# 776 instead of 756 score tiles on VectorE, with buffer rings that run on and a new written order

## The chip, the cores and the metric

The kernel runs on one core of a Trainium2 chip. The metric is device time in microseconds (us) of the whole program, as the median of several runs. The core has five engines that run their own instruction lists and wait for each other by semaphores: TensorE (PE in the profile, its weight loads PEld), VectorE (DVE), ScalarE (ACT), GpSimd (POOL) and SyncE (SP, which here only issues transfers).

## The reference

Two attention branches read the same input `x` of 2048 rows and 512 columns, with 32 heads of 16 dimensions. A gate `g = sigmoid(sum(x * gate_w))` per row mixes them.

```
A:  q,k,v = split(x @ wqkv);  pq = q @ w_phi;  pk = k @ w_phi        (per head)
    phi = concat(softmax(p), softmax(-p))
    o = phi_q @ (phi_k^T v) / (phi_q . sum(phi_k));   a = o @ wo      (linear attention)
B:  q,k,v = split(x @ wqkv);  p = softmax(q k^T / 4);  b = (p v) @ wo (full attention)
out = g * a + (1 - g) * b
```

Nearly all the time goes into B: for each of 32 heads a 2048 x 2048 score matrix, its exponential, and the product with `v`.

## The kernel before, in words

**Tiles and blocks.** B is cut into 32 blocks. A block is 512 query rows of four heads, which lie in four 32-row strips of the TensorE array. A block has 4 x 16 = 64 score tiles of 128 keys by 512 queries, 2048 tiles in all. TensorE makes a tile with one matmul (line 994: rows in the profile say `psS<-qz_t,kTB_t`, 32 rows by 128 columns of the array) into one of seven PSUM banks. Tiles of different heads use different row strips and stream together. The product with `v` (line 1136, `psO<-...,vaug_t`) uses 128 rows by 32 columns of the array; four of these on different column strips stream together into the bank `psO`. I call matmuls that stream together a round.

**Two ways to the exponential.** ScalarE takes two tiles at a time (line 1115, `E_t<-psS`, 128x1024) with its own exp; a tile then costs one product matmul. The other way is VectorE's: `max(s + EXPB, 0)` is written as a 16-bit integer (line 1084 for one tile, line 1074 for a pair of tiles in one instruction), and these bits, read as bf16, are a rough power of two. To smooth it, GpSimd adds a constant to all the integers, four at a time in a 64-bit add (line 1060, `INT64_ADD`), and later another one, and TensorE accumulates the product with `v` three times: of the first bits (`t`), of the first sum (`s`) and of the second (`m`). A tile on VectorE thus costs three product matmuls instead of one, and a quarter of two GpSimd adds, since up to four tiles form a group. `DN` (line 31) says how many tiles of each block go this way; there are 756, in 198 groups.

**Buffers.** A group uses a buffer for `t` and one for `s` and `m`. `PHASES` (line 32) lists rings of such buffers for three phases, from blocks 0, 16 and 27 on: `x0`, `x1` are halves of `Tx_t`, `y0`, `y1` of `Ty_t`, `a0` to `a3` lie in `vA_t`, `n0` in `WAT_t`, `wk`, `wq` in `Wp_t`, `wv` in `WB_t`. The loop behind it (lines 684 to 692) deals the buffers out in turn and starts at the ring's first buffer in each phase. A buffer can be written again when the TensorE matmuls that read it are done.

**The rest** is laid between: projections (line 754: 32 columns, line 842 and 855: V), branch A (transposes of line 1417, the two-operand VectorE operations `EA_t<-EA_t,ratio_t` of line 1444, `kzbd_t` of line 1473), each block's normalisation (copy of line 1231, small transfers by SyncE, `oT_t<-Tf_t,Rb_t` of line 1247), and the output projections at the end.

**The order** of each engine's instructions is written out by hand as numbers in `TABLE` (line 83), made offline; `Plan.place` (line 476) puts the operations in that order, gives each score tile the PSUM bank that `"homes"` names, and joins the VectorE operations of `"pairs"`. A -1 in TensorE's list is a filler: four matmuls with zero weights that add nothing (line 1126, `psO<-xT_t,zero_t`).

## Time and profile before

| | before |
|---|---|
| median of 3 runs, us | 659.53 (659.16 to 659.58) |
| profiled execution: span from first to last instruction, us | 657.6 |
| busy share PE / ACT / DVE / POOL, % | 99 / 97 / 93 / 62 |
| granted TensorE clock | 1.000 |
| exponentials of two tiles on ScalarE | 643 |
| VectorE score operations, single / pair | 638 / 59 |
| filler matmuls | 92 |

The span is one execution; the median contains 1.9 us more around it. PE's busy time counts each matmul until its modelled end, so that 99% says that matmuls follow each other closely, and not that the array streams all the time. How densely it streams is read from the starts of rows in the timeline.

### The profile page before, as it was taken

How to read it: one execution, taken by the hardware profiler on the slowest of the kernel's cores; microseconds unless marked ns; L12 is line 12 of the kernel's file. 1: busy time of each engine (PE TensorE's matmuls, PEld its weight loads, DVE VectorE, ACT ScalarE, POOL GpSimd, SP SyncE). 2: the span in 40 equal slices, each digit the busy share in tenths (PEclk: the TensorE clock that was granted, in tenths of full speed). 3: DMA queues.
4: the chain of work that ended last, by engine and by line, in shares of the span. 5: the costliest groups of instructions: out<-in, count | busy, mean ns of one | idle time of the engine just before them, and what ended most of it. 6: DMA issues, size and time to landing. Idle time of an engine off the chain costs nothing.

```text
span 657.6 us, 20651 instructions
## 1 busy us (share of the span) xinstructions
PE 649.1 (99%) x8820; PEld 227.3 (35%) x8820; DVE 609.4 (93%) x963; ACT 635.1 (97%) x720; POOL 410.8 (62%) x437
## 2 busy tenths in 40 slices
PE   8999999999999999999999999999999999999997
PEld 4333333434333333333233233322333333332333
DVE  6999899999998789999999999999999989999985
ACT  6999999999999999999999999999989999999996
POOL 7575367465665446486467876575867566656853
PEclk9999999999999999999999999999999999999999
DMA  6530101001010000000012431233211633134132
GB/s 131 104 100 12 33 12 27 11 11 19 11 27 10 16 18 8 19 17 14 23 37 47 100 77 33 63 78 68 48 51 35 102 56 83 35 63 103 44 84 48
DMA packets 67947, 30.94 MB, mean 47 GB/s; under 512 B 53208, under 2 KB 62808, under 8 KB 67856
## 3 DMA queue, kind: packets, MB, share of 16 engines
q1 hardware_dynamic: 65840, 28.82, 19.6%
q8 instruction: 69, 1.13, 0.7%
q10 hardware_dynamic: 1632, 0.79, 0.5%
q14 instruction: 22, 0.18, 0.1%
q0 software_dynamic: 384, 0.02, 0.1%
HBM read 7.87 MB, written 8.88 MB: 25 GB/s over the span
## 4 chain that ended last, share of the span: by engine, by line
PE 85%; DVE 12%; ACT 1%; issue 1%; DMA 1%; SPq 0%; DVEq 0%
PE psO L1136 32%; PE psS L994 30%; PE psS L754 15%; DVE Tx_t L1084 3%; PE psS L1417 3%; DVE Ty_t L1084 1%; DVE oT_t L1084 1%; DVE Wp_t L1084 1%; PE psS L842 1%; ACT E_t L1115 1%; DVE Tz_t L1084 1%; PE psS L1514 1%; PE psS L855 1%; PE psO L1126 1%; DMA phiK_t<-in_A_x_dram 1%
## 5 line engine op out<-in xcount | busy, mean ns | idle before, releaser
L1115 ACT ACTIVATE E_t<-psS 128x1024 bf16<-128x1024 f32 x643 | 601.9, 1068 | 11.2 <-PE psS L994 10.3
L994 PE MATMUL psS<-qz_t,kTB_t 32*128 32x512 bf16 (+1 forms) x2054 | 267.5, 383 | 2.8 <-ACT E_t L1104 0.6
L1084 DVE TENSOR_SCALAR Tx_t<-psS 128x512 int16<-128x512 f32 x246 | 163.2, 682 | 10.5 <-PE psS L994 9.4
L994 PEld LDWEIGHTS psS<-qz_t,kTB_t 32*128 32x128 bf16 x2054 | 71.8, 91 | 226.4 <-ACT E_t L1115 102.9
L1136 PE MATMUL psO<-E_t,vaug_t 128*32 128x512 bf16 x1292 | 119.0, 384 | 0.0
L1060 POOL INT64_ADD vA_t<-vA_t x72 | 71.6, 999 | 19.0 <-PE psO L1136 13.7
L1084 DVE TENSOR_SCALAR Ty_t<-psS 128x512 int16<-128x512 f32 x114 | 76.5, 682 | 4.8 <-PE psS L994 4.5
L1060 POOL INT64_ADD Ty_t<-Ty_t x42 | 44.0, 1048 | 18.5 <-PE psO L1136 18.1
L1060 POOL INT64_ADD Ty_t<-Tx_t x29 | 30.1, 1038 | 39.0 <-DVE Tx_t L1084 32.7
L1136 PE MATMUL psO<-vA_t,vaug_t 128*32 128x512 bf16 (+1 forms) x520 | 52.6, 384 | 0.0
L1136 PE MATMUL psO<-Ty_t,vaug_t 128*32 128x512 bf16 x440 | 45.4, 384 | 0.0
L1136 PEld LDWEIGHTS psO<-E_t,vaug_t 128*32 128x32 bf16 x1292 | 30.2, 95 | 39.5 <-issue 28.4
L1084 DVE TENSOR_SCALAR oT_t<-psS 128x512 int16<-128x512 f32 x62 | 41.7, 682 | 1.5 <-PE psS L994 1.0
L1084 DVE TENSOR_SCALAR Tz_t<-psS 128x512 int16<-128x512 f32 x60 | 40.2, 680 | 2.1 <-PE psS L994 1.8
L1060 POOL INT64_ADD vA_t<-Tx_t x22 | 22.7, 1032 | 31.0 <-DVE Tx_t L1084 24.1
L1060 POOL INT64_ADD phiQT_t<-Tx_t x19 | 18.9, 993 | 29.1 <-DVE Tx_t L1084 28.0
L1084 DVE TENSOR_SCALAR vA_t<-psS 128x512 int16<-128x512 f32 x54 | 36.2, 682 | 0.7 <-PE psS L994 0.3
L1084 DVE TENSOR_SCALAR WAT_t<-psS 128x512 int16<-128x512 f32 x52 | 35.2, 682 | 1.4 <-PE psS L994 1.2
L754 PE MATMUL psS<-Wp_t,xT_t 128*32 128x512 bf16 x512 | 35.8, 382 | 0.0
L754 PE MATMUL psS<-xT_t,WB_t 128*32 128x512 bf16 x480 | 34.9, 382 | 0.2
L1084 DVE TENSOR_SCALAR Wp_t<-psS 128x512 int16<-128x512 f32 x50 | 33.8, 683 | 0.9 <-PE psS L994 0.7
L1060 POOL INT64_ADD WoB_t<-oT_t x19 | 19.3, 1016 | 20.7 <-DVE oT_t L1084 16.5
(165 smaller groups left out, 920.1 us busy)
## 6 DMA issues: line engine op xcount, KB each, us to landing
dpq<-EA_t SPq DMA_DIRECT2D x16, 256.0 KB, 2.3
Rb_t<-lr SPq DMA_DIRECT2D x120, 32.0 KB, 1.9
dpo<-kv_t SPq DMA_DIRECT2D x16, 128.0 KB, 1.8
qz_t<-qz_t SPq DMA_DIRECT2D x120, 16.0 KB, 1.8
Tf_t<-Tf_t SPq DMA_DIRECT2D x60, 32.0 KB, 2.0
WB_t<-in_B_wqkv_dram SPq DMA_DIRECT2D x3, 384.0 KB, 3.6
out_dram<-WvA_t SPq DMA_DIRECT2D x8, 128.0 KB, 2.0
out_dram<-WB_t SPq DMA_DIRECT2D x6, 128.0 KB, 2.0
```

The costliest lines, as they stand in the source:

```text
L754: ins = e.matmul(out[32 * i:32 * i + 32, :], lhsT=lhsT[:, 32 * i:32 * i + 32], rhs=rhs, start=start, stop=stop, tile_position=(0, 32 * i))
L842: mms = [lambda e, ap, i=i, t=t: e.matmul(ap[:, 128 * i:128 * (i + 1)], lhsT=xT[:, t, NQ * c + 128 * i:NQ * c + 128 * (i + 1)], rhs=W_B[:, ...
L855: mms = [lambda e, ap, i=i, t=t: e.matmul(ap[:, 256 * i:256 * (i + 1)], lhsT=xT[:, t, NQ * c + 128 * (2 * hf + i):NQ * c + 128 * (2 * hf + ...
L994: return e.matmul(bank, lhsT=kT_B[32 * i:32 * i + 32, ROW[b // 2] % 2, 128 * kt:128 * (kt + 1)], rhs=qz[32 * i:32 * i + 32, b // 2 % 4, b ...
L1060: op = P.add("pool", P64 + W64 * size, d_prio(g["ts"][0]) - 5.0 + (0.0 if key == "s" else M_LATE), lambda e: e.int64_add(words(dst), words ...
L1084: ops.append(drain(f, mm, "dve", 0.70, d_prio(d), lambda e, ap, q=q: e.tensor_scalar(quarter(tb, q).bitcast(I16), ap, EXPB, 0.0, op0=ALU.a ...
L1115: op = P.add("act", EXP_OVH + 0.4267 * n, 0.0, lambda e: e.activation(Ebuf[:, j // 2 % EPAIRS, 512 * SZ[0] * (j % 2):512 * SZ[0] * (j % 2) ...
L1126: ins = e.matmul((psO if bank is None else bank)[32 * i:32 * i + 32, :], lhsT=zero[:], rhs=xT[:, 0, 0:NQ], start=bank is not None, stop=ba ...
L1136: return e.matmul(psO[32 * i:32 * i + w, :], lhsT=vaug[:, kt, o:o + w], rhs=rhs, start=start, stop=stop, tile_position=(0, 32 * i), skip_g ...
L1417: mms = [lambda e, ap, n=n, f=f: e.matmul(ap[:, 64 * n:64 * n + 64].rearrange("p (s g j) -> p s g j", s=2, j=4), lhsT=ident[:], rhs=es[n][ ...
L1514: mms = [lambda e, ap, g=g: e.matmul(ap[:, 64 * g:64 * g + 64], lhsT=qT(g)[:, 128 * j:128 * (j + 1)], rhs=kzbd[:, g, 0:64], start=True, st ...
```

## The change

Ten entries of `DN` grow by two, so that 20 more tiles go to VectorE (776 in 202 groups) and ten two-tile exponentials leave ScalarE. The rings no longer start anew with each phase: a group's place continues from the count of the phase before. All of `TABLE` is written anew; the title's last point, VectorE's operations with two operands in SBUF laid apart from GpSimd's adds, is in these numbers and in no other line of code.

```diff
-DN = (16, 24, 18, 24, 26, 26, 26, 20, 22, 22, 24, 18, 26, 24, 20, 26, 30, 22, 24, 26, 22, 24, 30, 26, 18, 22, 36, 18, 24, 24, 32, 16)
+DN = (16, 24, 18, 26, 26, 26, 28, 20, 22, 24, 24, 18, 28, 24, 20, 26, 32, 22, 26, 26, 22, 26, 30, 26, 20, 22, 36, 20, 24, 24, 34, 16)
...
+TURNS = (0, 0)
...
-    count = [0] * len(PHASES)
+    count, at = [0] * len(PHASES), [(0, 0)]
     for n, g in enumerate(groups):
         g["n"], g["ph"] = n, max(k for k in range(len(PHASES)) if g["ts"][-1]["t"][0] >= PHASES[k][0])
         rt, rs = PHASES[g["ph"]][1:]
         k = count[g["ph"]]
+        if g["ph"] == len(at):
+            more = count[g["ph"] - 1] - TURNS[g["ph"] - 1]
+            at.append(tuple((a + more) % len(ring) for a, ring in zip(at[-1], PHASES[g["ph"] - 1][1:])))
         count[g["ph"]] += 1
-        g["t"], g["s"] = rt[k % len(rt)], rs[k % len(rs)]
+        g["t"], g["s"] = (ring[(k + a) % len(ring)] for a, ring in zip(at[g["ph"]], (rt, rs)))
...
 TABLE = {
     "sp": (
-        0, 17, 2, 4, 5, 6, 7, 8, 10, 9, 11, 13, 14, 12, 15, 22, 26, 23, 27, 24, 25, 28, 29, 21, 132, 19, 967, 133, 968, 30, 20, 1094,
+        0, 17, 2, 4, 5, 6, 7, 8, 10, 9, 11, 12, 26, 13, 14, 15, 22, 21, 25, 28, 27, 24, 23, 30, 29, 19, 20, 132, 967, 133, 968,
...
```

What the new numbers do is seen in the built order. Instruction counts of the whole program that differ:

| | before | changed |
|---|---|---|
| ScalarE exponentials of two tiles | 643 | 633 |
| VectorE score operations, single / pair | 638 / 59 | 688 / 44 |
| GpSimd adds of four tiles / of two | 360 / 36 | 372 / 32 |
| product matmuls of 512 columns | 3560 | 3600 |
| filler matmuls | 92 | 0 |
| rounds of 512-column matmuls on TensorE | 2089 | 2065 |
| changes of the array's division (row strips, column strips, whole) between neighbours | 1215 | 1239 |

In the changed program code lines stand 14 to 17 further down (994 is 1011, 1136 is 1153, 754 is 768, 1060 is 1077, 1084 is 1101, 1417 is 1434).

First place, TensorE: the stretch before the transposes (`EA_t,ident_t`) of the fourth quarter of branch A's first query chunk. Before:

```order
L1136 MATMUL psO<-Tx_t,vaug_t 32x512 x4
L1136 MATMUL psO<-vA_t,vaug_t 32x512 x4
L994 MATMUL psS<-qz_t,kTB_t 128x512 x3
L1126 MATMUL psO<-xT_t,zero_t 32x512 x8
L994 MATMUL psS<-qz_t,kTB_t 128x512 x3
L1136 MATMUL psO<-Wp_t,vaug_t 32x512 x4
L1136 MATMUL psO<-vA_t,vaug_t 32x512 x4
L994 MATMUL psS<-qz_t,kTB_t 128x512 x4
L1136 MATMUL psO<-vA_t,vaug_t 32x512 x4
L994 MATMUL psS<-qz_t,kTB_t 128x512 x3
L1417 MATMUL psS<-EA_t,ident_t 128x64 x16
```

The same transposes in the changed program:

```order
L768 MATMUL psS<-xT_t,WB_t 32x512 x4
L1011 MATMUL psS<-qz_t,kTB_t 128x512 x4
L1153 MATMUL psO<-E_t,vaug_t 32x512 x6
L1153 MATMUL psO<-vA_t,vaug_t 32x512 x8
L1011 MATMUL psS<-qz_t,kTB_t 128x512 x3
L1531 MATMUL psS<-kzbd_t,phiQT_t 128x64 x4
L1531 MATMUL psS<-kzbd_t,WAT_t 128x64 x4
L1011 MATMUL psS<-qz_t,kTB_t 128x512 x2
L1531 MATMUL psS<-kzbd_t,phiQT_t 128x64 x4
L1531 MATMUL psS<-kzbd_t,WAT_t 128x64 x4
L1434 MATMUL psS<-EA_t,ident_t 128x64 x16
```

The filler pair (`zero_t`, two rounds) is gone, as are all 23 filler rounds, and other branch-A work stands close to the transposes; TensorE still alternates between score matmuls and products.

Second place, GpSimd: the first adds of the groups around block 27, where the third phase begins (a row names the buffer written and the one read; with different names it is a group's first add). Before:

```order
L1060 ISA vA_t<-Tx_t 128x1024 x2
L1060 ISA vA_t<-vA_t 128x1024
L1060 ISA WB_t<-Ty_t 128x2x256
L1060 ISA vA_t<-vA_t 128x1024 x3
L1060 ISA Ty_t<-Tx_t 128x1024
L1060 ISA vA_t<-WAT_t 128x1024
L1060 ISA vA_t<-vA_t 128x1024
L1060 ISA WB_t<-WB_t 128x2x256
L1060 ISA vA_t<-Tx_t 128x1024
```

Changed:

```order
L1077 ISA vA_t<-Wp_t 128x1024
L1077 ISA vA_t<-Tx_t 128x1024
L1077 ISA vA_t<-vA_t 128x1024 x2
L1077 ISA Wp_t<-WAT_t 128x4x256
L1077 ISA WB_t<-Tx_t 128x4x256
L1077 ISA Wp_t<-Wp_t 128x4x256
L1077 ISA Ty_t<-vA_t 128x1024
L1077 ISA WB_t<-WB_t 128x4x256
```

Before, the two last groups of block 26 and the two first of block 27 use both halves of `Tx_t`: each half comes up again two groups later, where the ring otherwise gives it back after six. Changed, the ring goes on with `Wp_t`, `Tx_t`, `Tx_t`, `WAT_t`, and each half comes up after six groups.

26 lines of the change are left out of this document (13 added, 13 removed), and 513 rows, old and new, of the table TABLE.

## The prediction

> **What bounds the kernel now.** I read the page's busy times first, then TensorE's timeline, since a busy share near 100% on three engines does not say which one sets the time.
>
> ```profile
> span 657.6 us, 20651 instructions
> PE 649.1 (99%) x8820; PEld 227.3 (35%) x8820; DVE 609.4 (93%) x963; ACT 635.1 (97%) x720; POOL 410.8 (62%) x437
> ...
> PE 85%; DVE 12%; ACT 1%; issue 1%; DMA 1%; SPq 0%; DVEq 0%
> ```
>
> The third row is the chain of work that ended last: 85% of it is TensorE, 12% VectorE, 1% ScalarE. GpSimd has room. What TensorE's share is made of shows in its timeline (start, length, what):
>
> ```profile
> 224.22 0.39 PE L1136 MATMUL psO<-oT_t,vaug_t 128*32 128x512 bf16 x4
> 224.43 0.39 PE L754 MATMUL psS<-Wp_t,xT_t 128*32 128x512 bf16 x4
> 224.65 0.39 PE L1136 MATMUL psO<-Tx_t,vaug_t 128*32 128x512 bf16 x4
> 224.97 0.39 PE L994 MATMUL psS<-qz_t,kTB_t 32*128 32x512 bf16 x3
> 225.29 1.12 PE L1417 MATMUL psS<-phiK_t,ident_t 128*128 128x64 bf16 x32
> 226.35 0.39 PE L994 MATMUL psS<-qz_t,kTB_t 32*128 32x512 bf16 x3
> ```
>
> Rounds of the same division of the array (rows of 128\*32) start 0.21 to 0.22 apart: 224.22, 224.43, 224.65. Where the next row divides it otherwise (128\*32 to 32\*128, or to 128\*128), the start comes after 0.32: 224.65 to 224.97 to 225.29. So a round is worth 0.22 and a change of division 0.10 more. The order of before holds 2089 rounds of 512 columns and 1215 changes: 2089 x 0.22 = 459.6 and 1215 x 0.10 = 121.5, together 581. The short matmuls come on top: 512 transposes in 16 runs of 32 at 1.06 each (225.29 to 226.35 above) are 17, and the V projections are 8 runs each of two kinds:
>
> ```profile
> 125.51 1.00 PE psS L842 x16
> ...
> 252.60 0.98 PE psS L855 x8
> ```
>
> These are 16 more; the small sums and products of branch A I estimate at 12 from their number. That is about 626 of 657.6. TensorE streams for 95% of the span with no waits counted, and under 30 is left for ramp, end and waits together. ScalarE is close behind:
>
> ```profile
> 93.16 19.52 ACT L1115 ACTIVATE E_t<-psS 128x1024 bf16<-128x1024 f32 x21
> ...
> L1115 ACT ACTIVATE E_t<-psS 128x1024 bf16<-128x1024 f32 x643 | 601.9, 1068 | 11.2 <-PE psS L994 10.3
> ```
>
> 21 exponentials in 19.52 with the last at its full 1.07: (19.52 - 1.07) / 20 = 0.92 from one to the next. ScalarE's idle time before them is 11.2 in all, and 10.3 of it ended with TensorE's scores. Among neighbours this tight TensorE leads: it is what ScalarE waits for, and it is the chain.
>
> **The change part by part.**
>
> *TensorE.* The fillers go:
>
> ```profile
> L1126 PE MATMUL psO<-xT_t,zero_t 128*32 128x512 bf16 x92 | 9.3, 384 | 0.0
> ...
> 423.28 0.62 PE L1126 MATMUL psO<-xT_t,zero_t 128*32 128x512 bf16 x8
> 423.83 0.45 PE L994 MATMUL psS<-qz_t,kTB_t 32*128 32x512 bf16 x3
> 424.21 0.40 PE L1136 MATMUL psO<-Wp_t,vaug_t 128*32 128x512 bf16 x4
> ```
>
> 92 are 23 rounds. Two of them hold the array from 423.28 to 423.83, which is 0.23 + 0.32, a round and a round with a change: the full price, with no idle time of TensorE ahead of the scores that follow. So these rounds are removed from a stream, 23 x 0.22 = 5.1. Against it stand 40 more product matmuls (20 tiles at three instead of one), ten rounds, and one more since a half-filled pair came in: 11 x 0.22 = +2.4. The same 2042 full score matmuls fall into 12 rounds fewer, -2.6. The divisions change 24 times more, 24 x 0.10 = +2.4. Sum: (-23 + 11 - 12) x 0.22 + 2.4 = -5.3 + 2.4 = **-2.9**. Bounds: if the fillers stood in time that TensorE would have waited anyway, the sum is -2.9 + 5.1 = +2.2 of work, paid out of waits; if the changes of division hide behind waits, it is -5.3. I take -2.9, since the row shows fillers paid in full.
>
> *ScalarE* loses ten exponentials, 10 x 0.92 = -9.2, from 635.1 to about 626. It gains nothing by itself as long as it waits for TensorE. If it set the pace everywhere the change would be worth up to 9.2.
>
> *VectorE* pays for it:
>
> ```profile
> 563.73 2.50 DVE L1084 TENSOR_SCALAR Tx_t<-psS 128x512 int16<-128x512 f32 x4
> ...
> 554.17 1.22 DVE L1074 TENSOR_SCALAR Wp_t<-psS 128x1024 int16<-128x1024 f32 x1
> 555.30 0.68 DVE L1247 TENSOR_TENSOR oT_t<-Tf_t,Rb_t 128x512 bf16<-128x512 f32 x1
> ```
>
> Single tiles follow each other at (2.50 - 0.68) / 3 = 0.61, and a pair holds it from 554.17 to 555.30, 1.13. 50 singles more and 15 pairs fewer: 50 x 0.61 - 15 x 1.13 = 30.5 - 17.0 = +13.5, or 0.42 for each of the 32 blocks. Its idle time of 657.6 - 609.4 = 48.2 covers that, but not evenly:
>
> ```profile
> 140.00:180.00 40.00, 39.87 (x592) 14.96 (x584) 39.51 (x59) 38.96 (x45) 24.49 (x28) 1.00 0.08 17
> ...
> 220.00:260.00 40.00, 40.00 (x566) 14.92 (x565) 34.49 (x51) 39.91 (x50) 21.65 (x26) 1.00 0.07 16
> 260.00:300.00 40.00, 39.83 (x543) 15.42 (x545) 39.06 (x60) 38.08 (x42) 24.43 (x26) 1.00 0.08 17
> 300.00:340.00 40.00, 39.08 (x528) 12.81 (x520) 38.66 (x65) 39.85 (x45) 26.24 (x26) 1.00 0.08 22
> 340.00:380.00 40.00, 39.92 (x526) 12.65 (x526) 39.05 (x61) 39.34 (x46) 28.50 (x29) 1.00 0.31 72
> 380.00:420.00 40.00, 39.88 (x552) 14.23 (x540) 38.72 (x62) 40.00 (x48) 27.15 (x27) 1.00 0.24 54
> ...
> 460.00:500.00 40.00, 39.87 (x557) 13.95 (x554) 38.80 (x63) 38.13 (x45) 29.02 (x30) 1.00 0.17 45
> ...
> 540.00:580.00 40.00, 39.88 (x559) 13.84 (x550) 38.94 (x63) 38.07 (x44) 25.32 (x26) 1.00 0.22 58
> ```
>
> (Columns: PE, PEld, DVE, ACT, POOL busy, then clock and DMA.) From 220 to 260 VectorE has 5.5 free of 40, but from 140 to 180 only 0.5, and from 260 to 300 and 340 to 380 0.9 each, where two blocks' addition is 0.84. I take 0 for the cover, with +4.1 for the whole program as the other end (worked out below as a rival).
>
> *GpSimd* gets 12 adds of four tiles and loses 4 of two:
>
> ```profile
> 557.88 0.61 POOL L1060 INT64_ADD WB_t<-Ty_t  x1
> ...
> 551.52 1.03 POOL L1060 INT64_ADD WB_t<-WB_t  x1
> ...
> 548.12 1.40 POOL L1060 INT64_ADD vA_t<-Wp_t  x1 [1.82 <-DVE Wp_t L1084]
> ...
> 547.93 0.68 DVE L1444 TENSOR_TENSOR EA_t<-EA_t,ratio_t 128x512 bf16<-128x512 bf16 x1
> ```
>
> 12 x 1.03 - 4 x 0.61 = +9.9 on 410.8, hidden in its 247 of idle time.
>
> *Two-operand operations apart.* The last two rows are a collision: the add at 548.12 begins while `EA_t<-EA_t,ratio_t` runs, and takes 1.40 instead of 1.03. GpSimd can afford that. VectorE pays in few places:
>
> ```profile
> L1247 DVE TENSOR_TENSOR oT_t<-Tf_t,Rb_t x15: 675/681/1200, 74.4 to 635.4; 128x512 bf16<-128x512 f32 x15
> ...
> 328.87 0.97 DVE kzbd_t L1473
> ```
>
> Of 15 normalisations (min/median/max in ns) the median is at the minimum and one took 1200, 0.52 over. The second row, from the chain of waits, is `kzbd_t`'s one operation, whose 0.97 stands against 0.60 between single-tile operations of equal size. At most 0.52 + 0.37 = 0.9 is to be had. I take **-0.4**, the part on the chain; 0 if the new order collides as often elsewhere. [...]
>
> *Rings.* At block 27 a `Tx_t` half is needed again after two groups instead of six. VectorE, which would wait for it, does not:
>
> ```profile
> 550.00:560.00 10.00, 9.88 (x142) 3.29 (x142) 10.00 (x14) 8.52 (x9) 8.09 (x9) 1.00 0.40 116
> ```
>
> It is busy all 10 of 10 there and TensorE 9.88, so TensorE can win 0.1; ScalarE's 1.5 of idle time ends up behind VectorE's own load. I take 0.
>
> Sum: -2.9 - 0.4 = -3.3, by the profiled execution 657.6 to 654.3. The median contains 1.9 more around the span, so **659.5 - 3.3 = 656.2**.
>
> **The rivals.** (1) *VectorE becomes the bound: slower.* Where it has no idle time left, each block grows by 0.42 instead of shrinking by 3.3 / 32 = 0.10. With n such blocks the change is 0.42 n - 0.10 (32 - n): zero at n = 6, and +1.3 at n = 9. The seven windows quoted with under 1.4 of 40 idle hold 14 blocks, at 20.5 each: 5.9 - 1.8 = +4.1, so 663.6. For it: VectorE's 12% of the chain. Against it: the new order may move VectorE's other work out of these stretches, and its whole idle time, 48.2, is 3.6 times the addition. (2) *ScalarE is the true bound: much faster.* Then all of 9.2 counts, 650.3. For it stand its 97%; against it, its idle time is ended by TensorE and it has 1% of the chain. [...] The starts above, 0.22 and 0.32 apart without gaps, speak against it. (3) *Nothing to be measured:* the fillers stood where waits now open, and TensorE's additional 2.2 is paid from ScalarE's slack, within 1.3 of 659.5. For it: behind the two fillers at 423.28 the product of 424.21 starts 0.38 after its scores instead of 0.32, so a wait of 0.06 follows them all the same. Against it: 0.06 is little beside 0.45. That the separation does not happen at all is part of it: it costs 0.4.
>
> **How the numbers follow.** Forecast 0.54, with its own range 654.2 (-5.3) to 658.2 (a gain of 1.3); rival 1 0.17; rival 2 0.08; rival 3 0.21. About 0.2% (1.3) can be told from no change. Faster: 0.54 + 0.08 = 0.62; same 0.21; slower 0.17. The range 652.0 to 661.5 leaves out most of rival 2 and over half of rival 1.
>
> **What would show it.** Right: the same 0.22 and 0.32 in TensorE's timeline, no `zero_t` rows, TensorE still over 80% of the chain, VectorE's busy time near 623 and ScalarE's near 626, no add of GpSimd over 1.1. Wrong: VectorE's share of the chain well over 12% with windows at 39.5 of 40 (rival 1); score matmuls waiting for VectorE where fillers stood (rival 3); TensorE idle and a gain near 9 (rival 2).

## The result: 8.6 us slower

| | before | changed |
|---|---|---|
| median, us | 659.56 (659.16 to 660.84) | 668.18 (667.01 to 671.1) |
| ratio to before | | 1.0132, 95% interval 1.0106 to 1.0159 |
| profiled execution, span, us | 657.6 | 665.0 |
| mean granted clock | 1.000 (profiled execution) | 1.000, 0.997, 0.995, 0.990 (the four timed executions; the first is the profiled one) |

The forecast was 656.2, the range 652.0 to 661.5. The time lies above both, and above the 663.6 of the rival on VectorE. The page of the changed kernel (span, busy times, the chain of work that ended last, the exponentials):

```profile
span 665.0 us, 20578 instructions
PE 649.9 (98%) x8768; PEld 228.1 (34%) x8768; DVE 620.9 (93%) x998; ACT 630.4 (95%) x710; POOL 422.6 (64%) x445
...
PE 66%; DVE 11%; SPq 10%; ACT 7%; DMA 3%; issue 1%; DVEq 0%
...
L1132 ACT ACTIVATE E_t<-psS 128x1024 bf16<-128x1024 f32 x633 | 595.4, 1042 | 23.6 <-PE psS L1011 22.7
```

TensorE's part of the chain falls from 85% to 66%. What takes its place is not VectorE (12% before, 11% now) but SyncE's queue (SPq, from 0 to 10%), ScalarE (1 to 7%) and the transfers themselves (1 to 3%). These shares tell where the path runs and not what a stretch costs: by line, 4 of SyncE's 10% are turned loads of the start (L696 and L706, loads that transpose on the way). ScalarE waits for scores twice as long as before, 23.6 instead of 11.2.

To see where TensorE lost time, I took the distance from each of its rounds to the next, and subtracted the lower quartile of the distances between rounds of the same kinds in the kernel before. The quartiles' sum is TensorE's work, the rest its waits. By this the work is 625.3 before and 622.5 now: -2.8, where -2.9 was forecast. The waits went from 27.8 to 38.0. Up to 400 us they are about the same (20.7 and 19.9). After 400 us, in us and by the engine that ended them:

| waits of TensorE after 400 us, ended by | before | changed |
|---|---|---|
| VectorE | 3.7 | 9.9 |
| ScalarE | 1.0 | 2.8 |
| a transfer | 0.0 | 1.8 |
| GpSimd | 0.1 | 1.4 |
| nothing that the trace shows | 2.3 | 2.2 |

VectorE's rise does not hang on how a wait is put down to an engine; GpSimd's does (by the releaser of each round's first matmul it has 0.3 before and now). Of these waits 0.9 is in pieces over 250 ns before, and 8.8 now. A few long waits are new. They are followed one by one.

**Transfers that land late.** The first two are at the start. TensorE's timeline of the changed kernel:

```profile
32.11 0.38 PE L1393 MATMUL psS<-Wbp_t,WAT_t 128*128 128x128 bf16 x4 [1.71 <-DMA WAT_t<-in_A_wqkv_dram]
...
35.26 0.38 PE L1393 MATMUL psS<-Wbp_t,WAT_t 128*128 128x128 bf16 x4 [0.92 <-DMA WAT_t<-in_A_wqkv_dram]
```

These products need the eight turned loads of `WAT_t` (`DMA_TRANSPOSE` in the rows). SyncE issues one after the other; seven of the eight stand here. Its queue in the changed kernel:

```profile
20.08 1.26 SPq L706 DMA_TRANSPOSE WAT_t<-in_A_wqkv_dram  x1
21.39 0.58 SPq L703 DMA_DIRECT2D WB_t<-in_B_wqkv_dram  x1
22.01 8.41 SPq L706 DMA_TRANSPOSE WAT_t<-in_A_wqkv_dram  x5
30.47 0.58 SPq L708 DMA_DIRECT2D WvA_t<-in_A_wqkv_dram  x1
31.10 1.19 SPq L706 DMA_TRANSPOSE WAT_t<-in_A_wqkv_dram  x1
```

and in the kernel before, where all eight stand together and the first product came 4 us later:

```profile
18.84 11.41 SPq L692 DMA_TRANSPOSE WAT_t<-in_A_wqkv_dram  x8
```

In the changed kernel two loads that nobody waits for yet stand between them, and the products were moved ahead.

The second half has the other ones. A block's row sums travel from VectorE's copy of the result (`Tf_t<-psO`) through memory (`ld`, then `Lq_t`) back to VectorE's reciprocal, and that one's result through memory again (`lr`, then `Rb_t`) to the scaling. Blocks are normalised in pairs. Pair 25 in the kernel before, VectorE first, then SyncE's queue:

```profile
535.85 0.68 DVE L1231 COPY Tf_t<-psO 128x512 f32<-128x512 f32 x1
543.80 0.34 DVE L1240 RECIPROCAL rd_t<-Lq_t 128x32 f32<-128x32 f32 x1
555.30 0.68 DVE L1247 TENSOR_TENSOR oT_t<-Tf_t,Rb_t 128x512 bf16<-128x512 f32 x1
```

```profile
536.56 0.53 SPq L1233 DMA_DIRECT2D ld<-Tf_t  x1
538.28 0.34 SPq L1235 DMA_DIRECT2D Lq_t<-ld  x1
...
544.17 0.38 SPq L1242 DMA_DIRECT2D lr<-rd_t  x1
...
547.08 5.03 SPq L1244 DMA_DIRECT2D Rb_t<-lr  x8
```

And in the changed kernel:

```profile
538.19 0.68 DVE L1248 COPY Tf_t<-psO 128x512 f32<-128x512 f32 x1
...
544.67 0.35 DVE L1257 RECIPROCAL rd_t<-Lq_t 128x32 f32<-128x32 f32 x1 [0.97 <-issue]
...
557.32 0.81 DVE L1264 TENSOR_TENSOR oT_t<-Tf_t,Rb_t 128x512 bf16<-128x512 f32 x1 [1.38 <-DMA Rb_t<-lr]
```

```profile
537.66 1.85 SPq L913 DMA_DIRECT2D qz_t<-qz_t  x3
539.56 1.26 SPq L1506 DMA_TRANSPOSE phiQT_t<-dpq  x1
540.92 0.53 SPq L1250 DMA_DIRECT2D ld<-Tf_t  x1
541.51 1.13 SPq L1506 DMA_TRANSPOSE phiQT_t<-dpq  x1
542.68 0.57 SPq L1252 DMA_DIRECT2D Lq_t<-ld  x1
...
547.37 0.38 SPq L1259 DMA_DIRECT2D lr<-rd_t  x1
547.80 1.19 SPq L1506 DMA_TRANSPOSE WAT_t<-dpq  x1
549.03 1.25 SPq L1506 DMA_TRANSPOSE phiQT_t<-dpq  x1
550.33 5.26 SPq L1261 DMA_DIRECT2D Rb_t<-lr  x8
```

Before, `ld` is issued 0.03 after the copy, and `Lq_t` has landed 3.8 ahead of the reciprocal. Now `ld` stands 2.05 behind the copy's end: copies of `qz_t` and a turned read of `dpq`, whose user comes at 562, stand ahead of it, one more turned read ahead of `Lq_t`, and two more ahead of `Rb_t`. VectorE waits 0.97 and 1.38. (The first row says "issue" since the profile names no releaser; `Lq_t` landed at 544.59, 0.08 ahead of that row's start.) It waited for no transfer before. TensorE is held up behind it: from the scores at 544.71 to the next at 545.62 it takes 0.91, and from 557.45 to 558.79 it takes 1.34, of which the trace shows 0.53 and 0.95 as idle, both ended by VectorE's operations on score tiles (`vA_t`, L1101). It needs the banks of score tiles that VectorE had not got to.

For the whole list I compared each transfer's landing with the start of its first user on TensorE or VectorE; I call the time between them the margin. Leaving out the first 24 us, of SyncE's 214 transfers with such a user none lands less than 1.0 us ahead in the kernel before, and 20 do in the changed kernel, 10 of them less than 0.3. The counts depend on how a transfer is paired with its user: with only those users whose own tile the transfer writes they are 0 and 12. From the end of a pair's copy to its reciprocal the median is 7.3 us before (6.7 to 9.4) and 5.4 now (4.2 to 11.7).

### The profile page after: what moved, and what is told of

It is laid out like the page before. It is cut to its first block, busy times and chain, and to the rows that moved or that the text cites. A ratio compares the mean times of both kernels' runs of the same rounds, so it can differ in the third digit from the quotient of the medians.

```text
span 665.0 us, 20578 instructions
## 1 busy us (share of the span) xinstructions
PE 649.9 (98%) x8768; PEld 228.1 (34%) x8768; DVE 620.9 (93%) x998; ACT 630.4 (95%) x710; POOL 422.6 (64%) x445
## 4 chain that ended last, share of the span: by engine, by line
PE 66%; DVE 11%; SPq 10%; ACT 7%; DMA 3%; issue 1%; DVEq 0%
PE psO L1153 26%; PE psS L1011 23%; PE psS L768 12%; ACT E_t L1132 7%; DVE Tx_t L1101 3%; SPq L1506 2%; SPq L696 2%; PE psS L1434 2%; SPq L706 2%; PE psS L869 1%; SPq L1261 1%; DVE vA_t L1101 1%; DVE Ty_t L1101 1%; DVE WAT_t L1101 1%; DVE EA_t L1461 1%
## 5 line engine op out<-in xcount | busy, mean ns | idle before, releaser
L1132 ACT ACTIVATE E_t<-psS 128x1024 bf16<-128x1024 f32 x633 | 595.4, 1042 | 23.6 <-PE psS L1011 22.7
L1101 DVE TENSOR_SCALAR Tx_t<-psS 128x512 int16<-128x512 f32 x262 | 172.1, 681 | 4.9 <-PE psS L1011 4.2
L1153 PE MATMUL psO<-E_t,vaug_t 128*32 128x512 bf16 x1272 | 125.5, 384 | 0.0
L1101 DVE TENSOR_SCALAR Ty_t<-psS 128x512 int16<-128x512 f32 x116 | 77.5, 680 | 4.8 <-PE psS L1011 4.3
L1153 PE MATMUL psO<-vA_t,vaug_t 128*32 128x512 bf16 x534 | 53.1, 385 | 0.0
L1101 DVE TENSOR_SCALAR Tz_t<-psS 128x512 int16<-128x512 f32 x72 | 47.9, 680 | 1.2 <-PE psS L1011 0.6
L1101 DVE TENSOR_SCALAR oT_t<-psS 128x512 int16<-128x512 f32 x66 | 43.7, 682 | 1.0 <-PE psS L1011 0.6
L1101 DVE TENSOR_SCALAR vA_t<-psS 128x512 int16<-128x512 f32 x62 | 41.3, 679 | 0.6 <-PE psS L1011 0.4
L768 PE MATMUL psS<-Wp_t,xT_t 128*32 128x512 bf16 x512 | 40.9, 382 | 0.5 <-DMA dpq<-EA_t 0.5
L1101 DVE TENSOR_SCALAR Wp_t<-psS 128x512 int16<-128x512 f32 x58 | 38.9, 680 | 1.4 <-PE psS L1011 1.4
L1077 POOL INT64_ADD Ty_t<-Tx_t x24 | 24.0, 1002 | 23.9 <-DVE Tx_t L1101 23.4
L1101 DVE TENSOR_SCALAR WAT_t<-psS 128x512 int16<-128x512 f32 x52 | 34.7, 682 | 0.9 <-PE psS L1011 0.8
L1077 POOL INT64_ADD WoB_t<-oT_t x19 | 18.9, 996 | 22.3 <-DVE oT_t L1101 21.6
L1077 POOL INT64_ADD WoA_t<-Tz_t x19 | 20.2, 1063 | 15.0 <-DVE Tz_t L1101 11.4
L1077 POOL INT64_ADD vA_t<-Tx_t x22 | 22.0, 1002 | 11.7 <-DVE Tx_t L1101 11.5
```

Source lines behind the costliest of these rows:

```text
L768: ins = e.matmul(out[32 * i:32 * i + 32, :], lhsT=lhsT[:, 32 * i:32 * i + 32], rhs=rhs, start=start, stop=stop, tile_position=(0, 32 * i))
L1077: op = P.add("pool", P64 + W64 * size, d_prio(g["ts"][0]) - 5.0 + (0.0 if key == "s" else M_LATE), lambda e: e.int64_add(words(dst), words ...
L1101: ops.append(drain(f, mm, "dve", 0.70, d_prio(d), lambda e, ap, q=q: e.tensor_scalar(quarter(tb, q).bitcast(I16), ap, EXPB, 0.0, op0=ALU.a ...
L1132: op = P.add("act", EXP_OVH + 0.4267 * n, 0.0, lambda e: e.activation(Ebuf[:, j // 2 % EPAIRS, 512 * SZ[0] * (j % 2):512 * SZ[0] * (j % 2) ...
L1153: return e.matmul(psO[32 * i:32 * i + w, :], lhsT=vaug[:, kt, o:o + w], rhs=rhs, start=start, stop=stop, tile_position=(0, 32 * i), skip_g ...
```

## The experiments

The theories were: the load of VectorE (rival 1 of the prediction), SyncE's queue, the fillers (rival 3), and, after the first runs, the granted clock and the margins as a whole. Medians are of all timed executions; the mean granted clock of single executions is given where it matters, and "at the full clock" means 1.000. In 56 executions of the kernel before that clock was under 0.9985 once.

| run | median, us (lowest to highest) | ratio to before, 95% |
|---|---|---|
| e1 no fillers | 659.93 (658.6 to 661.1) | 0.9997, 0.9989 to 1.0006 |
| e2 VectorE's load on before | 671.21 (670.8 to 671.3) | 1.0170, 1.0157 to 1.0184 |
| e3 VectorE relieved | 671.15 (667.4 to 674.2) | 1.0177, 1.0151 to 1.0202 |
| e4 queue mended | 665.62 (660.5 to 666.1) | 1.0067, 1.0041 to 1.0093 |
| e5 start only | 670.40 (667.8 to 671.6) | 1.0156, 1.0133 to 1.0179 |
| e6 later queue only | 666.53 (663.4 to 668.9) | 1.0098, 1.0075 to 1.0120 |
| e7 fillers for the clock | 666.68 (663.9 to 673.7) | 1.0119, 1.0081 to 1.0156 |
| e8 queue and fillers | 665.07 (664.0 to 671.1) | 1.0094, 1.0064 to 1.0125 |
| e9 margins by hand | 667.54 (666.0 to 668.6) | 1.0115, 1.0101 to 1.0128 |
| e10 margins and fillers | 669.27 (667.5 to 674.4) | 1.0153, 1.0125 to 1.0180 |
| e11 margins taken from before | 665.56 (663.2 to 666.2) | 1.0084, 1.0071 to 1.0097 |
| e12 e9 with VectorE relieved | 666.59 (665.9 to 668.9) | 1.0108, 1.0095 to 1.0122 |
| e13 row-sum block in before | 662.24 (659.8 to 665.0) | 1.0028, 1.0013 to 1.0044 |
| e14 searched queue and fillers | 664.94 (664.5 to 666.2) | 1.0070, 1.0054 to 1.0086 |

### The fillers

e1, the kernel before without its fillers, one of 23 places (this diff and some later ones have the operations' names in place of `TABLE`'s numbers):

```diff
-  dq21.13.3.0, qk424, -1, dq21.13.0.0
+  dq21.13.3.0, qk424, dq21.13.0.0
```

> The kernel before with its 23 filler rounds struck from TensorE's written order and nothing else changed. The prediction's first term (each filler takes a whole round of TensorE's time, 23 x 0.22 us): 5.1 us less, about 654.4. The prediction's third rival (the fillers stood in time in which TensorE waited anyway): within 1.3 us of before, 658.2 to 660.9. The theories on what the change cost (VectorE's load, SyncE's queue) say nothing of this run.

No change: 0.9997, which with its interval is between 0.7 us faster and 0.4 slower. The answer of rival 3 holds. The prediction had read the full price from two fillers at 423.28; this is the same place in TensorE's timeline without them:

```profile
422.26 0.39 PE L994 MATMUL psS<-qz_t,kTB_t 32*128 32x512 bf16 x3
423.09 0.46 PE L994 MATMUL psS<-qz_t,kTB_t 32*128 32x512 bf16 x3 [0.43 <-ACT E_t L1115]
423.48 0.40 PE L1136 MATMUL psO<-Wp_t,vaug_t 128*32 128x512 bf16 x4
```

Between the two scores there were 0.87 (422.96 to 423.83) with the fillers and there are 0.83 without. A wait for ScalarE's exponential came into their place. By the count of the first section TensorE's work fell by 6.2 over the program, and its waits rose by 5.4. In 4 of the 11 executions the clock's mean was 0.997; the section on the clock comes back to that.

### VectorE's load

e2, the kernel before with 22 single score tiles worked twice:

```diff
+            def score(e, ap, q=q, twice=twice):
+                if twice:
+                    e.tensor_scalar(spare[:], ap, EXPB, 0.0, op0=ALU.add, op1=ALU.max)
+                return e.tensor_scalar(quarter(tb, q).bitcast(I16), ap, EXPB, 0.0, op0=ALU.add, op1=ALU.max)
```

> The kernel before with 22 single score tiles of VectorE worked twice, the second time into a spare tile that nobody reads: about 13.1 us more work on VectorE, in the order of before, with the same result and no other engine's list touched. Theory of VectorE's load (the prediction's first rival: with 0.42 us more for each block VectorE is the bound): 4 us or more slower, 663.5 to 672. Theory of SyncE's queue (the new order puts other transfers ahead of those that are waited for, and the load by itself costs little): less than 2 us slower, below 661.5.

11.6 us slower, for 12.1 more of VectorE's busy time (621.5). Its chain, and the row of the added operations:

```profile
PE 70%; DVE 27%; issue 1%; ACT 1%; DMA 1%; SPq 0%; DVEq 0%
...
L1091 DVE TENSOR_SCALAR spare_t<-psS 128x512 int16<-128x512 f32 x22 | 15.0, 684 | 0.5 <-PE psS L994 0.5
```

VectorE's share rises from 12% to 27%. That answers the theory of the load, for this order: where the order isn't laid for it, VectorE's time is paid almost in full, and 48 us of idle time in sum cover 0.5 of 12.1. (The added operation stands ahead of the real one, so it also puts each of the 22 tiles off by some 0.6; load and delay are not told apart.) But the changed kernel has the same busy time (620.9) without this share in its chain. Its order was laid anew for the load, and so the other direction was to be tried on it.

e3, the changed kernel with 26 single tiles written for 64 of 512 queries:

```diff
-                quarter(tb, q).bitcast(I16), ap, EXPB, 0.0, op0=ALU.add, op1=ALU.max),
+                quarter(tb, q)[:, 0:w].bitcast(I16), ap[:, 0:w], EXPB, 0.0, op0=ALU.add, op1=ALU.max),
```

> The changed kernel, in its own order, with 26 of VectorE's single score tiles after the first 64 written for 64 of their 512 queries only (what the others of these tiles hold is left from before, so that part of the scores is left out): about 12 us less work on VectorE, every wait and transfer as it was. Theory of VectorE's load: the loss goes, 659 to 661. Theory of SyncE's queue: the waits for transfers stay, at most 2 us of the 8.6 come back, 666 or more.

671.15: nothing came back in the median, with 8.9 us less of VectorE's busy time (612.0; a short tile still takes 0.20 to 0.22, a full one 0.68). The clocks of its six executions are 0.984 to 0.995, lower than the changed kernel's, so some of what it gained may be hidden; e12 below repeats it on another basis. Even so the theory of the load as the one cause, which had 659 to 661, is not borne out.

### SyncE's queue

e4, the changed kernel with the written order mended (the numbers of `TABLE`; in SyncE's list 13 to 15 are loads of `x`, 22 to 29 those of `WAT_t`, 21 and 30 the two that were in between):

```diff
-  26, 13, 14, 15, 22, 21, 25, 28, 27, 24, 23, 30, 29, 19, 20
+  13, 14, 15, 22, 25, 24, 23, 26, 28, 27, 29, 21, 30, 19, 20
...
-  582, 3511, 581, 624, 626, 584, 583
+  582, 581, 584, 624, 626, 3511, 583
...
-  3645, 629, 3646, 628, 3647, 3649, 3650, 3822
+  3645, 3646, 3647, 3649, 629, 3650, 628, 3822
...
-  700, 3691, 4439, 701, 4568, 699, 4569, 4570, 4277, 4572, 705, 702, 4573
+  700, 4439, 701, 4568, 4569, 4570, 4572, 4573, 699, 705, 702, 3691, 4277
...
-  777, 4888, 772, 776, 773
+  777, 772, 776, 773, 4888
```

The second edit lets the scaled queries (624, 626) go ahead of a reordering of queries that is needed 80 us later; the third and fourth put the row sums of pairs 19 and 25 (3645 to 3650, 4568 to 4573) ahead of turned reads (628, 629, 699, 702, 705) and stores; the fifth puts a store behind turned reads. In TensorE's list product 243 moves behind 509 and 505, and VectorE's evictions follow.

> The changed kernel with SyncE's written order mended in five places and nothing taken out: at the start the six bias and weight loads that TensorE does not wait for stand behind the eight it does (and one of the weight products that need the last of these stands behind two that need the first four); in the second half the writes and reads of the row sums, the gathers of the merged outputs and the writes of the scaled queries stand ahead of the transposes and stores that nobody waits for yet. VectorE's work is as in the changed kernel. Theory of SyncE's queue: the five stalls of TensorE that the trace of the changed kernel puts down to transfers (2.9 us at the start, 0.7, 0.5, 0.9, 1.3 and 1.1 us later) go, 6 to 8 us less, 660 to 662. Theory of VectorE's load: VectorE was late anyway and its other waits take their place, at most 2 us less after the start's 2.9, 663 or more.

Its trace has none of these waits for transfers any more. The executions fall into two groups: 660.53 and 661.98 at a clock of 1.000, and 665.4 to 666.1 at 0.988 to 0.995. At the full clock it is 5.0 to 6.5 below the changed kernel's 667.01, what SyncE's theory forecast, and within 0.4% of the kernel before. The median, 665.62, is 2.6 below. So two things seem to work here; the second is the clock.

e5 has the first edit and TensorE's alone, e6 the four later ones:

> The changed kernel with the start alone mended: on SyncE the biases and the weight load that are not waited for stand behind the eight loads of the transposed weight, and the weight product that needs the last of them stands behind two that need the first four. Theory of SyncE's queue: the stalls of 1.87 and 0.99 us at 30 and 34 us go, and the executions at the full clock lie 2.9 us lower, at 664.1. If the start is made up for later (another engine is late anyway): within 1 us of the changed kernel's 667.0. The clock's theory (next run) says that the executions spread upwards by 2 to 5 us as those of the changed kernel do.

> The changed kernel with SyncE's order mended in the four later places alone (from 410 us on) and the start as it was. Theory of SyncE's queue: stalls of 0.7, 0.5, 0.9, 1.3 and 1.1 us go, the executions at the full clock lie 3.6 to 4.5 us lower, at 662.5 to 663.4. Theory of VectorE's load: VectorE is late at these places without the transfers too, less than 1.5 us. Together with the run before the two gains should come to the 6.5 us by which the fastest execution of the kernel with both lies below the changed kernel's fastest.

e6 at the full clock has 663.39, 3.6 less, as forecast. e5 has no execution at the full clock (0.989 to 0.994), so its time decides nothing. Its trace says more: TensorE is 2.2 us earlier than in the changed kernel from 36 us on and still at 382 us, and 2.7 earlier at 612. It loses 3.5 right after that: it waits 2.1 for the turned reads, 1.0 more than in the changed kernel, and then the clock is at half from 616 to 623. The start is not made up for by another engine, but a lead is no use where the next transfer is not earlier too.

All this sets single executions against a single one, the 667.01, and the same list is not equally late in each execution. e7 below has the SyncE list of the changed kernel, and at the full clock it has 663.88 and 667.11. In its profile neither operation of pair 25 waits:

```profile
543.24 0.34 DVE L1261 RECIPROCAL rd_t<-Lq_t 128x32 f32<-128x32 f32 x1
...
554.55 0.68 DVE L1268 TENSOR_TENSOR oT_t<-Tf_t,Rb_t 128x512 bf16<-128x512 f32 x1
```

At the start the last `WAT_t` lands at 35.12 in the changed kernel's profile, and at 33.44, 34.04 and 34.44 in those of e3, e6 and e7 with the same list there; with the mended one it lands at 31.13 and 31.30 (e4, e5). So the order of the list decides how late a transfer can be, and the execution how late it is. What the mended list is worth is therefore better read from all executions: the ratio is 1.0067 against 1.0132, and the intervals do not overlap (up to 1.0093, from 1.0106). That is about half of the loss, some 4 us.

### The granted clock

The profiled execution of e4 around its first group of row-sum products, the products of 4 columns with `kzbd_t` in branch A (columns: PE, PEld, DVE, ACT, POOL busy, then the clock and DMA):

```profile
384.00:388.00 4.00, 3.12 (x64) 1.60 (x56) 3.97 (x9) 3.09 (x4) 3.00 (x3) 1.00 0.19 38
388.00:392.00 4.00, 4.00 (x34) 0.70 (x32) 3.42 (x6) 3.51 (x4) 2.15 (x3) 0.65 0.28 88
392.00:396.00 4.00, 4.00 (x38) 0.71 (x34) 2.52 (x5) 2.53 (x4) 1.04 (x1) 0.50 0.46 138
```

The clock is at half for some 7 us, and only 34 to 38 matmuls start in 4 us, where the two windows of 4 us behind have 60 and 50. By the rows that is (0.35 + 0.50) x 4 = 3.4 us of full speed; by the starts of the same rounds TensorE lost 2.9 us there against the changed kernel's profile. In the 4 us ahead TensorE stands still for 0.9 in three pieces (0.40, 0.15, 0.33), and among the rounds between are 32 products of 4 columns. The changed kernel's own profiled execution has the same stretch at the full clock; its other executions have 0.990 to 0.997. The same fall shows in the profiles of e3, e6, e9 and e12, at 386 to 389, and others in e3, e5, e6 and e10 after 616, behind the wait for the last turned reads.

e7 puts fillers there (five around the first group, four in the wait ahead of the last), e8 puts them into e4:

```diff
+  -1, -1, 3306, 3462, 3370, 3464, 3304, -1, 563, 564, -1, 565, 566, -1, 3467
-  3306, 3462, 3370, 3464, 3304, 563, 564, 565, 566, 3467
```

> The changed kernel with nine filler rounds (0.22 us each, all zeros, the same as those of the kernel before) put into the stalls around two groups of rounds that hardly stream: five around the first group of row-sum products at 384 to 387 us, where TensorE waits 0.40, 0.15 and 0.33 us between rounds of 4 columns, four in the stall of 1.1 us before the last group at 616 us. SyncE's order as in the changed kernel. Theory of the clock (the granted clock falls to half for some 7 us when a stretch of about 3 us holds too little streaming, as in the traces of the two last runs after 388 and after 619 us): no execution under a mean clock of 0.998 but for the start, and the executions lie close together at 667 +- 1. If the fall of the clock has another cause: the same spread from 667 to 671 with clocks of 0.990 to 0.995.

> The changed kernel with SyncE's order mended at the start and in the later places, and seven filler rounds around the first and the last group of row-sum products. If late transfers and the fallen clock are all that this order lost against its own full-clock demand: 660.0 to 661.5 in nearly all executions, level with the kernel before at 659.6 to within 0.3%. If the clock falls for another reason: the two groups of times seen without the fillers, near 661 and near 666.

In the profiles of all four runs with fillers at the first group (e7, e8, e10, e14) the clock does not fall there; in five of the seven profiles of the changed order without them it does. By the starts of the same rounds the five fillers cost TensorE 0.46 us there in the profiles of e7, e8 and e14. But the spread stayed (0.987 to 1.000 in e7, 0.990 to 1.000 in e8), since it falls elsewhere: in e7 after a wait of 1.6 us for VectorE, ended at 590.8. And e8 is not level with the kernel before, as was expected: at the full clock it has 664.0 and 664.5. In its trace TensorE waits 1.5 us for a copy of the queries at 44 us (`qe0.1`), which landed 0.7 ahead of its user in the profile of the changed kernel, and 0.8 at 647 us for a turned read. The executions are late at different places.

e13 asks the question by itself, in the kernel before:

```diff
-  Z0.0, dq19.15.1.0, qk390, Z0.8, Z0.16, Z0.24, dq19.14.2.0, qk391, -1
+  Z0.0, Z0.8, Z0.16, Z0.24, dq19.15.1.0, qk390, dq19.14.2.0, qk391
```

(three more -1 within 15 us of it are struck out too).

> The kernel before with the first group of row-sum products (four rounds of 4 columns, at 397 us) in one piece, as the changed kernel has it, instead of one round, two other rounds and three, and with the four filler rounds around it struck out; all else as before. Theory of the clock (a stretch with little streaming at this place makes the granted clock fall to half for some 7 us): in at least a third of the executions a mean clock of 0.995 to 0.997 and 2 to 4 us more, the others at 659.7. If the block and the fillers have nothing to do with it: all executions at 0.999 or more and 659.7 +- 0.5, as those of the kernel before.

Ten of twelve executions have a clock of 0.992 to 0.997 and 661.4 to 665.0, and the two others 659.8 and 659.9. That is what the theory of the clock had said. The profile shows the place, and for comparison the same stretch of the kernel before:

```profile
402.00:406.00 4.00, 3.22 (x27) 0.99 (x31) 3.83 (x8) 3.67 (x5) 2.25 (x2) 0.60 0.01 2
406.00:410.00 4.00, 4.00 (x57) 1.23 (x45) 3.10 (x5) 2.98 (x5) 2.17 (x3) 0.97 0.05 12
```

```profile
402.00:406.00 4.00, 4.00 (x61) 1.33 (x53) 4.00 (x6) 4.00 (x6) 2.27 (x3) 1.00 0.04 10
406.00:410.00 4.00, 4.00 (x55) 1.12 (x54) 4.00 (x6) 4.00 (x5) 3.43 (x4) 1.00 0.35 113
```

In these 8 us the clock lacks (0.40 + 0.03) x 4 = 1.7 us of full speed. The run changes the block and four fillers together. e1 answers this in part: with all fillers out and the block as it was, the clock is 0.997 in 4 of 11 executions, against one in 56 with the fillers. So taking fillers out is part of it, and fillers, which the prediction had as a cost alone, also held up the clock here. The profile has a second fall, at 7 to 14 us, where e4's has one too.

What sets the clock was not shown. In all nine profiles that have a fall (e3 to e7, e9, e10, e12 and e13) the lowest clock of any 2 us is 0.50. The stretch of about 3 us in e7's expectation is, in e4's trace, the one that holds the three pieces, 384.44 to 387.32; how long such a stretch must be, or how little TensorE must do in it, was not measured.

### The margins

e11 takes from the kernel before what the changed one lacks. Only VectorE's list changes, pair 19 for example:

```diff
-  ev.19 and 12 others, rd19
+  ev.19 and 7 others, rd19, the 5 others
```

> The kernel before with one thing changed: the reciprocal of the row sums stands two to six places earlier on VectorE in thirteen of the fifteen pairs of blocks, so that it comes about 5.2 us after the eviction that its input sets out from, the distance that the changed kernel has, instead of 7.3. All engines' work, all transfers and their order as before. Theory of the margins: VectorE waits for the landing in some of the pairs (1 to 2 us in pair 19, under 1 us in 23, what the landings vary by in others), 1 to 3 us slower with a wider spread, 660.5 to 663. If the transfers' margins do not matter: within 0.7 us of the kernel before.

5.9 us slower, twice the upper end of what I expected, and 3.5 to 4.2 at the full clock (663.19 and 663.87). VectorE's wait at pair 19 (its `Lq_t` landed 0.08 ahead of the row's start), and TensorE's behind it:

```profile
427.70 0.35 DVE L1244 RECIPROCAL rd_t<-Lq_t 128x32 f32<-128x32 f32 x1 [1.94 <-issue]
```

```profile
428.66 0.64 PE L1421 MATMUL psS<-EA_t,ident_t 128*128 128x64 bf16 x16 [1.92 <-DVE Tx_t L1088]
```

1.94 of VectorE become 1.92 of TensorE: there is no cover on the way. Three of five executions have a clock of 0.995 to 0.997; that these falls follow the late transfers is not shown, since the profiled execution has none. This run moves only small operations by 2 to 4 us, with the load, the transfers and their order as they were.

e9 was to give the changed kernel margins, by hand, e10 the fillers too, and e12 repeats the relief of e3 on e9 (26 single tiles written for 64 of 512 queries):

```diff
-  ld0, qe0.1, lq0
+  qe0.1, ld0, lq0
...
-  (VectorE) rd23, three others
+  (VectorE) the three others, rd23
```

(two of some sixty such moves).

> The changed kernel with the start mended and SyncE's whole list from 33 us on written out anew, each transfer as early as those that are needed sooner allow, and the reciprocal of the row sums moved one to three places later on VectorE in eleven of the fifteen pairs of blocks (the scaling of pair 5 as well, three places), so that hardly a transfer lands less than 0.7 us before its first user (20 of 214 land less than 1.0 us before it in the changed kernel, none after the start in the kernel before). Engines' work, TensorE's order and the banks as in the run with the queue mended. Theory of the margins (the new order left the transfers no time to be late in): nearly all executions between 659 and 662, the median level with the kernel before to within 0.3%, and fewer falls of the clock, since these follow stalls. If the mended places were the whole loss: two groups as before, near 661 and 666.

> The run before with five filler rounds around the first group of row-sum products at 384 to 387 us, where TensorE waits for other engines (not for a transfer) three times before and after rounds that hardly stream. If that place is where the clock still falls: no mean clock under 0.998, 659 to 661.5 throughout. If it falls elsewhere or not at all: as the run before, within 0.5 us.

> The kernel of the first of these runs (margins restored) with 26 of VectorE's single score tiles written for 64 of their 512 queries only (the rest of these scores is left out), about 12 us less work on VectorE. Theory of VectorE's load as a second term beside the transfers: 3 us or more lower than with the full work, below 658. If the load lies in VectorE's waits in this order: within 1.5 us of it.

None of the three came out as the theory of the margins had it. The transfers that land less than 1.0 ahead went from 20 to 14 in e9, not to none: from the end of a pair's copy to the start of its scaling the changed VectorE order has 17.2 us in the median (15.6 at pair 19), where there were 18.9 before (18.5), and e9 has 16.4; within that, moving the reciprocal later only takes from `Rb_t` what it gives to `Lq_t`. And all ten executions of e9 and e10 have a fallen clock. The new list has a fault of its own: it puts a write of scaled queries behind the eight transfers of `Rb_t`. e9 and e12, with the same list, do not wait for it in their profiles, where the clock is at half just there. e10 does, and its clock falls behind that wait, at 398:

```profile
396.94 0.40 PE L774 MATMUL psS<-Wp_t,xT_t 128*32 128x512 bf16 x4 [2.10 <-DMA dpq<-EA_t]
```

e12 is 0.9 us below e9, with 10.9 us less of VectorE's busy time (621.9 to 611.0). Their intervals overlap, and by the outer ends at most some 2 us of the 10.9 can have come back, so VectorE's load as such is not what this order mainly pays for.

e14 orders SyncE's list from 33 us on by a search for the largest margins, with e9's list for VectorE, the fillers of e7's first place and three more ahead of the last group:

> The changed kernel with the start mended, SyncE's list ordered by a search for the largest margins between a transfer's landing and its first user (at the latencies that 85 of 100 transfers in the traces keep), the reciprocals one to three places later, five filler rounds around the first group of row-sum products and three before the last. Theory of the margins and the clock together: fewer executions with stalls over 1 us than in the two runs that were ordered by hand, median 661 to 664, the best near 660. If margins of 5.2 us between eviction and reciprocal cannot be kept by any order of SyncE's list, since VectorE's own order sets them: as those, 666 to 669.

664.5 to 666.2, the narrowest group of the changed order's variants, five of six at 0.999 or 1.000. The first stretch of e4's fence is now at the full clock:

```profile
384.00:388.00 4.00, 4.00 (x71) 1.95 (x68) 3.62 (x8) 3.03 (x4) 3.21 (x4) 1.00 0.23 48
388.00:392.00 4.00, 4.00 (x51) 1.06 (x49) 3.96 (x7) 4.00 (x5) 1.93 (x2) 1.00 0.30 86
```

So the clock was held here, and e14 is still 0.7% slower than the kernel before. Nine transfers land less than 1.0 ahead. By the count of the first section TensorE waits 15.9 us after 400 us (18.1 in the changed kernel, 7.1 before), 9.9 of it ended by VectorE. No variant of the changed order beats the kernel before.

**What stays open.** Three things were seen. Late transfers: about half of the loss goes with e4's list, and reciprocals nearer to their inputs alone cost 5.9 (e11). The clock: up to 4 us more in the changed kernel's executions in which it fell. And waits that belong to the written order: after 400 us, six waits stand at the same rounds with the same length in all eleven profiles of the changed order, whatever was done to the queue, the load or the fillers. Four are ended by VectorE (0.36 behind a tile at 459 us, 0.53 behind `statq_t` at 511, 0.48 behind a tile at 535, 0.50 behind the last `oT_t` at 661) and two by ScalarE (0.35 and 0.33), 2.5 in sum; the kernel before has two over 0.3 there, 0.8 in sum. The second of them, in the changed kernel and in e14:

```profile
511.34 0.60 PE L1011 MATMUL psS<-qz_t,kTB_t 32*128 32x512 bf16 x4 [0.25 <-DVE statq_t L1442]
```

```profile
509.56 0.60 PE L1017 MATMUL psS<-qz_t,kTB_t 32*128 32x512 bf16 x4 [0.26 <-DVE statq_t L1448]
```

(The scores ahead of them start 0.64 earlier; 0.11 is the lower quartile for neighbours of these kinds.) What this does not explain is e14, whose executions at the full clock (664.5 to 666.2) are above e4's two (660.5 and 662.0). By the starts of the same rounds in the two profiles, that is spread over pieces of 0.3 to 0.7 at 163, 387 (the five fillers), 442, 592, 601, 617 and 650 us, and no single change accounts for them. TensorE's waits that VectorE ends stay at 8.1 to 9.9 after 400 us in e4, e12 and e14, against 3.7 before, with the load and without 11 us of it; but for the four above, which operations of VectorE the new order puts too late was not isolated. The rings alone were not tried either, since the order that is written for the one kind of rings does not fit the other. (The loop that deals the rings' buffers out stands at line 965 of the kernel before, not at 684 to 692.)

## Why the prediction was wrong

Two steps failed. The 5.1 us of the fillers were taken as time, and they were none. And the waits of before were taken as unchanged (cover 0, rings 0, no term for SyncE's transfers), where TensorE's waits rose by 10.2. With the work of -2.8 that makes the 7.4 us by which the span grew.

*TensorE, -2.9.* As work it was right: 625.3 to 622.5, with rounds 0.22 and changes 0.32 apart as before. As time it was not, and the reason is in the first part of the sum, 5.1 for the fillers. "With no idle time of TensorE ahead of the scores that follow" was read from a row in which the filler itself filled that time. e1 measured it: nothing, between 0.7 us gained and 0.4 lost. Without that term the sum is -2.9 + 5.1 = +2.2, the other end that the prediction had written down.

*VectorE, cover 0.* This is one half of the second step. The busy time rose by 11.5 (forecast 13.5). Of the sign named for rival 1, windows at 39.5 of 40 busy, the changed kernel comes close. Two windows before, and the same two now:

```profile
420.00:460.00 40.00, 39.55 (x503) 11.91 (x503) 36.83 (x61) 40.00 (x45) 25.14 (x25) 1.00 0.29 71
500.00:540.00 40.00, 39.98 (x535) 12.74 (x539) 38.16 (x62) 40.00 (x47) 23.36 (x25) 1.00 0.40 73
```

```profile
420.00:460.00 40.00, 39.22 (x497) 12.80 (x489) 39.36 (x63) 37.26 (x42) 26.08 (x27) 1.00 0.29 65
500.00:540.00 40.00, 39.43 (x486) 12.59 (x486) 39.39 (x67) 40.00 (x46) 26.62 (x26) 1.00 0.30 68
```

VectorE has 0.6 of 40 free there; before, these windows had 3.2 and 1.8. The other half of the sign, VectorE's share of the chain well over 12%, is not there (11%), and the sign for "right" of TensorE over 80% of the chain is not either (66%). Rival 1 had the side right and the price (+4.1) too small. (At n = 9 its formula gives +1.5 and not +1.3; nothing hangs on it.) Its mechanism is at most part of it: in an order that isn't laid for the load it costs 0.96 us for each us (e2), in the one that is, taking 9 to 11 us away gives nothing that can be told from no change (e3, e12). What can be pointed at in the denser order are the margins of transfers and the fixed waits above; that both come from its density is argued, not tested.

*The other half: SyncE was not costed at all.* The sum has terms for TensorE, VectorE, ScalarE, GpSimd, two-operand operations and rings. The change moves nearly every transfer in SyncE's list and the reciprocals towards their inputs, and no line of the prediction prices that or has it as a rival, though the before profile shows `Lq_t`, `Rb_t` and the turned reads. About half of the loss goes with e4's list, and the direct test on the kernel before (e11) gives 5.9 for the reciprocals alone. "Rings, I take 0" and "cover 0" took the waits of before as given.

*Two-operand operations, -0.4.* The two named cases went: the normalisation of 1200 ns (the longest is 807 now), and `kzbd_t`'s operation. Each had begun while an add of GpSimd ran, 0.38 and 0.53 behind the add's start. `kzbd_t`'s before and after:

```profile
L1473 DVE TENSOR_TENSOR kzbd_t<-kv_t,mask_t x1: 1054/1054/1054, 328.8 to 328.8; 128x512 bf16<-128x512 f32 x1
```

```profile
L1490 DVE TENSOR_TENSOR kzbd_t<-kv_t,mask_t x1: 682/682/682, 317.9 to 317.9; 128x512 bf16<-128x512 f32 x1
...
L1461 DVE TENSOR_TENSOR EA_t<-EA_t,ratio_t x16: 676/684/1420, 328.1 to 600.3; 128x512 bf16<-128x512 bf16 x16
```

But one `EA_t` scaling took 1420 ns now (the longest before was 707); it starts at 382.66, 0.16 behind the start of an add. And 13 adds of GpSimd exceed 1.1 us as 13 did before. All 13 of before begin while one of these two-operand operations runs, 0.12 to 0.49 behind its start, and 12 of the 13 now, 0.02 to 0.85 behind. That part of the change moved collisions and did not remove them.

*GpSimd and ScalarE.* GpSimd +11.8 (forecast 9.9), hidden as said, but for at most 1.4 us of waits after 400. ScalarE's busy time fell by 4.7, not 9.2: its exponentials by 6.5, while its other work rose by 1.8. Rival 2 would have had the time fall with ScalarE's load; it rose.

*Rival 3* had the fillers right (a wait for ScalarE opens where they stood, at 423.09 in e1) and the rest wrong: it took ScalarE's slack to pay for them.

## What to carry to other kernels

When an order of instructions is written anew, list for every transfer how long before its first user it lands, before and after; reciprocals 2 us nearer to their inputs cost 5.9 us here (e11) with all work as it was. One profile is one execution: the same list was late by 0.97 and 1.38 us at a place in one profile and on time in another (e7), so read what a queue costs from several. An operation that fills a wait is not worth its duration when removed: read what its successor waits for, not whether time is idle beside it. And an engine's idle time in sum (48 us) says nothing of what more load costs in a fixed order (11.6 for 12.1).

## What the runs showed of the hardware that I had not expected

TensorE's granted clock fell to 0.50 for some 3 to 10 us behind a stretch in which TensorE was idle for 0.9 us of 4, in pieces, with 32 products of 4 columns among the rounds between (e4; at the same place in e3, e6, e9 and e12), and behind single waits of 1.6 us (e7) and 2.1 us (e10). That the few columns have a part in it was not isolated. Whether the clock falls differs from one execution to the next of the same kernel (e4: 660.5 at 1.000, 666.1 at 0.995). With filler rounds of zeros at that place no fall was seen there in four profiles. They cost nothing measurable in the kernel before (e1), and 0.46 us for five of them in the changed order.
